# Attention feeding a dense network: another order of the first loads, of the first batch's products, and of the second batch's transposes

## The chip, the cores and the metric

The kernel runs on one core of a Trainium2 chip. Its engines are TensorE (PE in the profile; PEld is its weight load), VectorE (DVE), ScalarE (ACT), GpSimd (POOL) and SyncE (SP). All loads are issued from POOL, all stores from SP. The metric is the device time of one execution in microseconds, the median over the runs.

## The reference

For 8 batches, 8 heads, 576 positions and 64 channels a head, attention looks back over 32 positions. Heads 0 to 3 ("plain") see the last 32 positions, heads 4 to 7 ("dilated") every fourth of the last 128. The result goes, with heads side by side, through a dense network with a product of two branches.

```
rel = pos[:, None] - pos[None, :]
mask_plain = (rel >= 0) & (rel < 32)
mask_dil   = (rel >= 0) & (rel < 128) & (rel % 4 == 0)
scores = where(mask, q @ k.T / sqrt(64), -1e9)
attn = softmax(scores)
x = (attn @ v) as [8*576, 512]
out = ((x @ w1) * (x @ w2)) @ w3 @ w_out
```

w1 and w2 are 512 x 1024, w3 is 1024 x 1024, w_out is 1024 x 512.

## The kernel before

**Attention steps.** The work of a batch is cut into four steps (class Step): d0 and d1 are the two halves of the dilated heads (u = 1), p0 and p1 the two halves of the plain heads (u = 0). A step has three parts. The scores (L262 to L308): products of a k block (128 keys) with a q block (96 queries), then an exp on ACT into `et`. In the first batch the mask is added by a product with `ident` (L291); in the later ones DVE multiplies it in (L306). The values (L310 to L360): products of `et` with V, where V carries a column of ones, so that the sum of the softmax comes along; DVE takes the reciprocal (L325) and multiplies (L328) into `xo`. To channels (L366 to L388): six transposes on PE turn `xo` into the layout of the dense network, through a PSUM tile (`ps_x`, or a bank), and ACT or DVE copies that into `XT` (L388).

**q and k** come as rows. `load_qk` brings both halves u of a batch, or one; in the first batch each is a load of its own. DVE transposes them in 32 x 32 blocks (`transpose_qk`): four instructions (L247), or one for k of the plain heads (L240). Four of them take some 1.24 us.

**V** is loaded twice in two layouts: `vp` for the plain heads (one large load, and a small one of 12 KB for the first block, L130 and L131) and `vd` for the dilated heads (four loads, L140).

**The first batch** (`first_batch`, L415 to L446) is written out by hand, as nothing else can run beside it: each engine gets its instructions in the order of these lines. `scores_of_pair` and `values_of_pairs` work on two heads at a time, in two PSUM tiles `ps_s` and in banks of a pool of three (`bank()`). `begin` starts four of the dense network's products on the dilated channels of XT, which are ready first.

**The dense network and the later batches.** w3 and w_out are multiplied once into `wf_sb`: `fuse_t` transposes a block of w3 on PE and copies it to `w3T` (on DVE for odd blocks, on ACT for even ones, L593), `fuse_m` multiplies it (L601), and DVE writes the result to `wf_sb` (L609). `ffn1` (L515, L545, L546) makes the two branches for 512 tokens, `ffn2` (L571, L578) the output. Between them stand calls of `point()`, which count up. Sixteen lie in the first `ffn1` pass, two in each of the eight rounds of `fuse_m`, one ahead of each half. Steps of the second batch are due at given counts (`second_batch`, L450 to L475); those of later batches are spread evenly over the points. So instructions of a step lie in each engine's queue between those of the dense network, in the order of these calls.

**Loads** are issued in the order of the last lines of the program (L612 to L632): q, k and V of batch 0, then w1 and w2 in three parts, w3 in four, w_out in two, and the q, k and V of batch 1 among them. `const_pool` makes masks and the identity on POOL, so it stands in the same queue; `const_spread` copies masks on DVE.

Of the kernel before, what the change touches and what calls it, by code (L numbers as in the profile page):

```python
# [11 lines left out]
BF16 = mybir.dt.bfloat16  # L12
# [8 lines left out]
D = 64  # L21
# [15 lines left out]
def kernel(  # L37
# [11 lines left out]
    nc = tc.nc  # L49
# [22 lines left out]
    def four_banks():  # L72

        stage.close()
        return stage.enter_context(
            tc.tile_pool(name="psb", bufs=1, space=bass.MemoryType.PSUM)
        )
# [13 lines left out]
    NV = 3  # L91
# [8 lines left out]
    ps_x = psum.tile([P, 2 * TB], BF16, name="ps_x")  # L100
# [4 lines left out]
    def bank():  # L105
        return banks.tile([P, TB], F32, tag="f", name="f")
# [4 lines left out]
    def load_qk(b, us=slice(0, 2), which=(0, 1)):  # L111
        for nm, dst, src in [(("qn", qn, q), ("kn", kn, k))[i] for i in which]:
            if b not in dst:
                dst[b] = qk_pool.tile([P, 2, ROWS * D], BF16, tag=nm, name=nm)
            x = src[b].rearrange("(u h) (j a) d -> (h j) u (a d)", u=2, a=ROWS)
            nc.gpsimd.dma_start(out=dst[b][:, us], in_=x[:, us])  # L116

    def load_vp(b):
        vp = vps[b % NV]
        base = v[b, 0]  # L120

        def rows(p0, n, j0, nj):
            return bass.AP(
                tensor=base.tensor,
                offset=base.offset + (96 * j0 - 32 + p0) * D,
                ap=[[D, n], [96 * D, nj], [1, D]],
            )

        if b < NV:
            nc.gpsimd.dma_start(out=vp[32:P, 0:1, 0:D], in_=rows(32, 96, 0, 1))  # L130
            nc.gpsimd.dma_start(out=vp[:, 1:24, 0:D], in_=rows(0, P, 1, 23))  # L131
        else:
            nc.gpsimd.dma_start(out=vp[:, :, 0:D], in_=rows(0, P, 0, 24))

    def load_vd(b):


        x = v[b, 4]
        for m, p0, n, i0, second in ((0, 32, 96, 0, 0), (1, 0, 80, 64, 0), (1, 80, 48, 0, 1), (2, 0, P, 16, 1)):
            nc.gpsimd.dma_start(  # L140
                out=vds[b % 2][p0 : p0 + n, 4 * m : 4 * m + 4, 16 : 16 + 2 * D],
                in_=bass.AP(
                    tensor=x.tensor,
                    offset=x.offset + (4 * i0 + 2 * second) * D,
                    ap=[[4 * D, n], [S * D, 4], [1, 2 * D]],
                ),
            )
# [27 lines left out]
    def warm_up(n):  # L175

        ps = ps_x.bitcast(F32)
        for _ in range(n):
            nc.tensor.matmul(
                out=ps, lhsT=warm[:, 0:P], rhs=warm, start=True, stop=True  # L180
            )
# [19 lines left out]
    def const_pool():  # L201
        def keep(t, base, pattern, cm):
            nc.gpsimd.affine_select(
                out=t, in_=t, compare_op=AL.is_ge, fill=NEG,
                base=base, pattern=pattern, channel_multiplier=cm,
            )

        mp = mp0.rearrange("p (b a i) -> p b a i", b=2, a=2)
        keep(mp, 32, [[1, 2], [2, 2], [4, 24]], -1)
        keep(mp, -1, [[-1, 2], [-2, 2], [-4, 24]], 1)  # L210
        keep(md0, 32, [[1, 96]], -1)
        keep(md0, -1, [[-1, 96]], 1)
        make_identity(nc, ident, nomemset=True)
# [11 lines left out]
    def const_masks():  # L225
        for mask, neg in ((mask_pl, neg_pl), (mask_di, neg_di)):
            nc.vector.tensor_scalar(
                out=mask, in0=neg, scalar1=-1.0, scalar2=None, op0=AL.is_ge
            )


    def transpose_qk(b, u, which):


        src, dst = ((qn, qts), (kn, kts))[which]
        pad = PADK * which
        t = src[b][:, u, :].bitcast(U32).rearrange("p (a i) -> p a i", a=ROWS)
        o = dst[u][b % 2].rearrange("p s c -> p (s c)").bitcast(U32)[:, pad : pad + S]
        if u == 0 and which == 1:
            nc.vector.transpose(out=o.rearrange("p (j a) -> p a j", a=ROWS), in_=t)  # L240
            return
        for a0 in range(4):

            n = 5 - a0 // 2
            at = RES * SLOTS.index(a0)
            step = RES * SLOTS.index((a0 + 2) % 4) + (a0 + 18) // 4 - at
            nc.vector.transpose(  # L247
                out=bass.AP(
                    tensor=o.tensor,
                    offset=o.offset + at,  # L250
                    ap=[o.ap[0], [1, n], [9, 16], [step, 2]],
                ),
                in_=t[:, a0 : a0 + 4 * n - 3 : 4, :],
            )

    class Step:
# [80 lines left out]
        def new_xo(self):  # L337
            self.xo = wk_pool.tile([P, 2, 6, D], BF16, tag="xo", bufs=3, name="xo")

        def values_of_pairs(self):  # L340
            self.new_xo()
            products = []
            for hp in range(2):
                ov = bank()[:, 0 : 6 * (D + 1)].unsqueeze(1)
                ov = ov.rearrange("p n (j e) -> p n j e", e=D + 1)
                for m in range(3):
                    for hl in range(2):
                        self.value_matmul(2 * hp + hl, m, ov[:, 0, 2 * m + hl, :])
                products.append(self.normalize(ov, self.xo[:, hp], 1, 6))
            for f in products:  # L350
                f()

        def values(self):
# [47 lines left out]
    def prefetch(b):  # L401
        if b < B and b not in issued:
            issued.add(b)
            load_qk(b)
            load_vd(b)
            load_vp(b)

    def later(f, *args):
        phases.append([lambda: f(*args)])
# [5 lines left out]
    def first_batch():  # L415

        d0, d1, p0, p1 = steps[0:4]
        transpose_qk(0, 1, 0)
        transpose_qk(0, 1, 1)
        d0.scores_of_pair(0)  # L420
        d0.scores_of_pair(1)
        transpose_qk(0, 0, 0)
        d1.scores_of_pair(0)
        d1.scores_of_pair(1)
        d0.values_of_pairs()
        transpose_qk(0, 0, 1)
        d1.values_of_pairs()
        warm_up(4)
        p0.scores_of_pair(0)
        p0.scores_of_pair(1)  # L430
        d0.to_channels(ps_x, nc.vector.tensor_copy)
        p1.scores_of_pair(0)
        p0.values_of_pairs()
        p1.scores_of_pair(1)
        d1.to_channels()
        p1.values_of_pairs()
        pool = four_banks()
        ps_b = [pool.tile([P, TB], F32, name=f"ps_b{i}") for i in range(4)]
        begin(0, 0, ps_b[0])
        begin(0, 1, ps_b[1])  # L440
        p0.to_channels()
        begin(1, 0, ps_b[2])
        p1.to_channels(bank().bitcast(BF16), nc.vector.tensor_copy)
        begin(1, 1, ps_b[3])
        const_masks()
        prefetch(2)  # L446
# [3 lines left out]
    def second_batch():  # L450

        d0, d1, p0, p1 = steps[4:8]
        for at, f, *args in (
            (19, transpose_qk, 1, 1, 0),
            (20, transpose_qk, 1, 1, 1),
            (22, d0.scores),
            (24, d1.scores),
            (26, d0.values),
            (26, transpose_qk, 1, 0, 0),
            (27, transpose_qk, 1, 0, 1),  # L460
            (28, d0.to_channels),
            (28, d1.values),
            (30, p0.scores),
            (30, d1.to_channels),
            (32, p1.scores),
            (34, p0.values),
            (36, p0.to_channels),
            (36, p1.values),
            (36, prefetch, 3),
            (36, transpose_qk, 2, 1, 0),  # L470
            (38, p1.to_channels),
            (38, transpose_qk, 2, 1, 1),
        ):
            later(f, *args)
            when.append(at)  # L475

    def segment(lo, hi):

        for i in range(lo, hi + 2):
# [12 lines left out]
            if st is not None:  # L492
# [11 lines left out]
                if at == 3 and more:  # L504
                    behind(transpose_qk, b + 1, 0, 0)

    second_batch()
    segment(8, 4 * B)

# [15 lines left out]
    def begin(f, i, ps):  # L525

        begun[f, i] = ps
        ffn1_half(0, f, (w1_sb, w2_sb)[i], (2, 3), begun[f, i])
# [83 lines left out]
    const_vector()  # L612
    warm_up(16)
    load_qk(0, 1)
    const_pool()
    load_qk(0, 0, (0,))
    load_vd(0)
    load_qk(0, 0, (1,))
    load_vp(0)
    load_w12(0, 256)  # L620
    load_w12(256, 512)
# [8 lines left out]
    load_w3(3)  # L630
    load_qk(1, 0)
    load_vp(1)  # L632
    const_spread()

    first_batch()


# [64 lines left out]
```

## Time and profile before

| What | us |
|---|---|
| Median of 8 runs | 262.91 (262.44 to 264.09) |
| The profiled execution, its own time | 263.7 |
| Its span, first to last instruction | 261.9 |
| PE busy, of the span | 249.3 (95%) |
| DVE busy | 159.1 (61%) |
| ACT busy | 111.9 (43%) |
| Products of the dense network, first branch pair (L515) | 128.9 |
| Products of its output (L571) | 66.3 |
| Load of q of batch 1, dilated heads: issue, time to landing | 20.74, 17.6 |
| Load of k of batch 1, dilated heads | 22.07, 17.7 |

How to read it: the time of an execution is some 1.8 us over its span. PE works nearly all of the time; most of its idle time lies in the first 22 us, where the first batch waits for its loads, and between 34 and 71 us. The loads are one long stream: many are issued well before the 16 DMA engines come to them, so that the time to landing is mostly queueing.

### The profile page before, as it was taken

The numbers are of one execution on the slowest core, as the hardware profiler recorded it, in microseconds if no ns is written. First come the engines' busy times: TensorE is split into PE (matmuls) and PEld (weight loads), VectorE is DVE, ScalarE is ACT, GpSimd is POOL, SyncE is SP. The second block draws the span as 40 slices with busy tenths as digits, with TensorE's granted clock in tenths as the row PEclk, the third lists the DMA queues.
The fourth block names the chain that finished last, engine by engine and source line by source line (L and its number), as shares of the span: only waits on it lengthen the run. The fifth ranks groups of instructions, "written<-read, shape, count | busy, mean of one in ns | idle before, by whom it ended". The sixth has DMA issues, their size and how long they took to land.

```text
span 261.9 us, 5673 instructions
## 1 busy us (share of the span) xinstructions
PE 249.3 (95%) x2343; PEld 127.2 (49%) x2380; DVE 159.1 (61%) x332; ACT 111.9 (43%) x166; POOL 57.8 (22%) x84
## 2 busy tenths in 40 slices
PE   7789989999899999999999999999999999999994
PEld 2454455555455555554555555555554554444442
DVE  6575356976988578857785777578746633312420
ACT  1343334254555455345545554555445323324332
POOL 8953235546261105112411320000000000000000
PEclk9999999999999999999999999999999999999999
DMA  6999999999999969974968591300140022014013
GB/s 102 169 190 209 207 211 201 189 188 224 235 203 138 158 178 91 109 127 135 114 94 134 136 98 39 116 11 4 40 122 0 3 80 80 0 53 111 0 38 122
DMA packets 51961, 30.50 MB, mean 116 GB/s; under 512 B 37984, under 2 KB 42336, under 8 KB 51936
## 3 DMA queue, kind: packets, MB, share of 16 engines
q0 software_dynamic: 46160, 20.70, 63.7%
q1 hardware_dynamic: 5776, 9.44, 11.3%
q8 instruction: 18, 0.29, 0.4%
q14 instruction: 7, 0.06, 0.1%
HBM read 41.39 MB, written 9.44 MB: 194 GB/s over the span
## 4 chain that ended last, share of the span: by engine, by line
PE 85%; DVE 6%; DMA 2%; issue 2%; POOL 2%; ACT 2%; POOLq 0%; ACTq 0%
PE f L515 45%; PE f L571 23%; PE ps_a L275 4%; PE ps_a L317 4%; PE f L601 3%; PE ps_x L374 3%; DMA vd<-in_v_dram 2%; DVE xo L328 1%; PE ps_b L515 1%; DVE kt L240 1%; DVE qt L247 1%; ACT et L305 1%; DVE et L306 1%; POOL vd L140 1%; PE ps_s L275 1%
## 5 line engine op out<-in xcount | busy, mean ns | idle before, releaser
L515 PE MATMUL f<-XT,w_sb 128*128 128x512 bf16 x538 | 128.9, 379 | 1.3 <-issue 0.2
L515 PEld LDWEIGHTS <-w_sb 128*128 128x128 bf16 x576 | 52.8, 98 | 58.0 <-DVE XT L388 0.6
L546 DVE TENSOR_TENSOR gt<-f,asb 128x512 bf16<-128x512 f32 x70 | 48.1, 687 | 39.8 <-PE f L515 35.5
L545 ACT CAST asb<-f 128x512 bf16<-128x512 f32 x70 | 40.9, 585 | 62.6 <-PE f L515 59.8
L571 PE MATMUL f<-wf_sb,gt 128*128 128x512 bf16 (+1 forms) x287 | 66.3, 373 | 1.0 <-issue 0.8
L578 ACT COPY osb<-f 128x512 f32<-128x512 f32 (+1 forms) x37 | 21.2, 573 | 49.0 <-PE f L571 48.7
L571 PEld LDWEIGHTS <-gt 128*128 128x128 bf16 x296 | 27.1, 98 | 27.6
L305 ACT ACTIVATE et<-ps_a 128x1152 bf16<-128x1152 f32 x28 | 31.7, 1134 | 13.4 <-PE ps_a L275 13.3
L140 POOL DMA_DIRECT2D vd<-in_v_dram x32 | 21.2, 669 | 43.0 <-PE ps_a L317 35.0
L328 DVE TENSOR_TENSOR xo<-ps_a,rcp 96x768 bf16<-96x768 f32 x28 | 26.7, 954 | 1.0
L247 DVE STREAM_TRANSPOSE qt<-qn 128x160 uint32<-128x160 uint32 (+1 forms) x64 | 19.6, 423 | 1.4 <-DMA qn<-in_q_dram 1.4
L317 PEld LDWEIGHTS <-et 128*128 128x128 bf16 x384 | 15.8, 98 | 7.8 <-DVE xo L328 0.7
L275 PEld LDWEIGHTS <-kt 32*128 32x128 bf16 x768 | 10.9, 93 | 16.5 <-issue 13.1
L306 DVE TENSOR_TENSOR et<-et,mask_pl 128x1152 bf16<-128x1152 bf16 x14 | 10.6, 759 | 11.7 <-ACT et L305 11.6
L306 DVE TENSOR_TENSOR et<-et,mask_di 128x1152 bf16<-128x1152 bf16 x14 | 10.6, 757 | 10.1 <-ACT et L305 10.0
L325 DVE RECIPROCAL rcp<-ps_a 96x12 f32<-96x12 f32 x28 | 6.3, 225 | 16.4 <-PE ps_a L317 16.4
L601 PE MATMUL f<-wo_sb,w3T 128*128 128x512 bf16 x60 | 15.4, 380 | 0.9 <-ACT w3T L593 0.7
L374 PEld LDWEIGHTS <-xo 96*128 96x128 bf16 x192 | 11.4, 97 | 7.2 <-DVE xo L328 0.3
L275 PE MATMUL ps_a<-qt,kt 32*128 32x96 bf16 x672 | 12.4, 202 | 1.8 <-DVE xo L328 1.5
L374 PE MATMUL ps_x<-ident,xo 96*128 96x96 bf16 x186 | 13.1, 206 | 0.0
L116 POOL DMA_DIRECT2D qn<-in_q_dram x10 | 6.6, 663 | 21.8 <-DVE qt L247 18.1
L388 ACT COPY XT<-ps_x 128x576 bf16<-128x576 bf16 x16 | 10.3, 644 | 1.5 <-PE ps_x L374 1.4
(61 smaller groups left out, 141.9 us busy)
## 6 DMA issues: line engine op xcount, KB each, us to landing
qn<-in_q_dram POOLq DMA_DIRECT2D x6, 576.0 KB, 8.5
kn<-in_k_dram POOLq DMA_DIRECT2D x6, 576.0 KB, 9.7
w3n<-in_moe_w_dram POOLq DMA_DIRECT2D x4, 512.0 KB, 16.2
vp<-in_v_dram POOLq DMA_DIRECT2D x5, 384.0 KB, 6.5
out_dram<-osb SPq DMA_DIRECT2D x7, 256.0 KB, 2.3
out_dram<-osb SPq DMA_DIRECT2D x8, 224.0 KB, 3.1
out_dram<-osb SPq DMA_DIRECT2D x8, 192.0 KB, 2.7
out_dram<-osb SPq DMA_DIRECT2D x8, 160.0 KB, 2.3
```

The costliest lines, as they stand in the source:

```text
L140: nc.gpsimd.dma_start(out=vds[b % 2][p0 : p0 + n, 4 * m : 4 * m + 4, 16 : 16 + 2 * D], in_=bass.AP(tensor=x.tensor, offset=x.offset + (4 * ...
L275: nc.tensor.matmul(out=bank_of(h)[:, c0 : c0 + 96], lhsT=kt[prt, 96 * m : 96 * m + P, c], rhs=rhs, start=(start and c == 0), stop=(c == 1 ...
L305: nc.scalar.activation(out=ev, in_=ps_a[:, :, 0:HALF], func=ACT.Exp, scale=scale)
L306: nc.vector.tensor_tensor(out=ev, in0=ev, in1=mk.unsqueeze(1).to_broadcast([P, 4, HALF]), op=AL.mult)
L317: nc.tensor.matmul(out=out, lhsT=self.et[:, c0 : c0 + P], rhs=rhs, start=True, stop=True)
L328: nc.vector.tensor_tensor(out=xo[0:96].rearrange("p (n k) d -> p n k d", n=n), in0=ov[0:96, :, :, x0 : x0 + D], in1=rcp[0:96].unsqueeze(3) ...
L374: nc.tensor.transpose(out=xo, in_=self.xo[0:96, hp, 2 * m : 2 * m + 2, :], identity=ident[0:96, 0:96],)
L515: nc.tensor.matmul(out=ps, lhsT=w_sb[:, c, f * P : (f + 1) * P], rhs=XT[:, c, t * TB : (t + 1) * TB], start=(c == 2), stop=(c == 1),)
L545: nc.scalar.copy(out=a_sb, in_=ps)
L546: nc.vector.tensor_tensor(out=gts[t][:, f], in0=pss[1], in1=a_sb, op=AL.mult)
L571: nc.tensor.matmul(out=y, lhsT=gts[t][:, f, tb * P : (tb + 1) * P], rhs=wf_sb[:, f, c0 : c0 + n], start=(f == 0), stop=(f == KFF - 1),)
L601: nc.tensor.matmul(out=wf_ps[ft], lhsT=w3T[ft][:, g, :], rhs=wo_sb[:, g, :], start=(g == 0), stop=(g == KFF - 1),)
```

## The change

Four things are changed.

1. In the program's first loads: before, q and k of the dilated heads, the masks, q of the plain heads, V of the dilated heads (four loads), k of the plain heads, V of the plain heads. After: q and k of the dilated heads, q of the plain heads, the masks, k of the plain heads, V of the dilated heads, V of the plain heads.
2. In `first_batch`: the transposes of the plain heads' k stand ahead of d1's scores, p0's first scores ahead of d0's values, and d1's values are done in two parts between the scores of p0 and p1. Four warm-up products are gone. d0's, d1's and p0's to_channels go through `ps_x` and ACT one after the other, where d0's copy was on DVE and to_channels stood between the scores before.
3. In `second_batch`: the transposes of q and k are due at a count one higher (19, 20 to 20, 21, and 26, 27 to 27, 28), and d1's to_channels at 31 instead of 30.
4. V of the plain heads is loaded in one piece instead of two for batches 1 and 2 too (as for the later batches before).

```diff
-        if b < NV:
+        if b == 0:
             nc.gpsimd.dma_start(out=vp[32:P, 0:1, 0:D], in_=rows(32, 96, 0, 1))
             nc.gpsimd.dma_start(out=vp[:, 1:24, 0:D], in_=rows(0, P, 1, 23))
         else:
...
+        def values_of_pair(self, hp):
+            if hp == 0:
+                self.new_xo()
+            ov = bank()[:, 0 : 6 * (D + 1)].unsqueeze(1)
+            ov = ov.rearrange("p n (j e) -> p n j e", e=D + 1)
+            for m in range(3):
+                for hl in range(2):
+                    self.value_matmul(2 * hp + hl, m, ov[:, 0, 2 * m + hl, :])
+            return self.normalize(ov, self.xo[:, hp], 1, 6)
+
         def values_of_pairs(self):
...
+            for f in [self.values_of_pair(hp) for hp in range(2)]:
                 f()
...
         transpose_qk(0, 0, 0)
+        transpose_qk(0, 0, 1)
         d1.scores_of_pair(0)
         d1.scores_of_pair(1)
+        p0.scores_of_pair(0)
         d0.values_of_pairs()
-        transpose_qk(0, 0, 1)
-        d1.values_of_pairs()
-        warm_up(4)
-        p0.scores_of_pair(0)
         p0.scores_of_pair(1)
-        d0.to_channels(ps_x, nc.vector.tensor_copy)
+        d1.values_of_pair(0)()
         p1.scores_of_pair(0)
+        d1.values_of_pair(1)()
+        p1.scores_of_pair(1)
         p0.values_of_pairs()
-        p1.scores_of_pair(1)
+        d0.to_channels()
+        p1.values_of_pairs()
         d1.to_channels()
-        p1.values_of_pairs()
+        p0.to_channels()
         pool = four_banks()
         ps_b = [pool.tile([P, TB], F32, name=f"ps_b{i}") for i in range(4)]
         begin(0, 0, ps_b[0])
         begin(0, 1, ps_b[1])
-        p0.to_channels()
+        p1.to_channels(bank().bitcast(BF16), nc.vector.tensor_copy)
         begin(1, 0, ps_b[2])
-        p1.to_channels(bank().bitcast(BF16), nc.vector.tensor_copy)
         begin(1, 1, ps_b[3])
...
-            (19, transpose_qk, 1, 1, 0),
-            (20, transpose_qk, 1, 1, 1),
+            (20, transpose_qk, 1, 1, 0),
+            (21, transpose_qk, 1, 1, 1),
             (22, d0.scores),
             (24, d1.scores),
             (26, d0.values),
-            (26, transpose_qk, 1, 0, 0),
-            (27, transpose_qk, 1, 0, 1),
+            (27, transpose_qk, 1, 0, 0),
+            (28, transpose_qk, 1, 0, 1),
             (28, d0.to_channels),
             (28, d1.values),
             (30, p0.scores),
-            (30, d1.to_channels),
+            (31, d1.to_channels),
...
     load_qk(0, 1)
+    load_qk(0, 0, (0,))
     const_pool()
-    load_qk(0, 0, (0,))
+    load_qk(0, 0, (1,))
     load_vd(0)
-    load_qk(0, 0, (1,))
     load_vp(0)
```

## The prediction

> **What bounds the kernel now.** I read the page's totals first, then the chain of waits, then the timeline of the two stretches that the diff touches: 0 to 22 us (first batch of attention, alone on the chip) and 36 to 53 us (second batch, laid between products of the weights).
>
> ```profile
> PE 249.3 (95%) x2343; PEld 127.2 (49%) x2380; DVE 159.1 (61%) x332; ACT 111.9 (43%) x166; POOL 57.8 (22%) x84
> DMA  6999999999999969974968591300140022014013
> ```
>
> PE is the bound on average, so a microsecond is won or lost only where PE stands still. The DMA row shows that the 16 engines have no pause until about 90 us (14 slices of 6.55): a load's landing time is set by its place in the stream, not by when its user wants it.
>
> The chain of waits in the first stretch, and the timeline's ends of it:
>
> ```profile
> 6.48 5.63 DMA vd<-in_v_dram
> ...
> 13.69 1.17 DVE kt L240
> ...
> 21.99 1.90 PE ps_b L515 x8
> ```
>
> ```profile
> 12.15 0.59 PE L317 MATMUL f<-vd,et 128*128 128x65 bf16 x14 [0.31 <-DMA vd<-in_v_dram]
> 13.61 1.25 DVE L240 STREAM_TRANSPOSE kt<-kn 128x576 uint32<-128x576 uint32 x1
> 16.98 0.54 PE L317 MATMUL f<-vp,et 128*128 128x65 bf16 x12
> 19.48 0.98 DVE L328 TENSOR_TENSOR xo<-f,rcp 96x384 bf16<-96x384 f32 x2
> 21.98 11.77 PEld L515 LDWEIGHTS <-w_sb 128*128 128x128 bf16 x56 [0.61 <-DVE XT L388]
> ```
>
> To be seen: the last V load of the dilated heads lands at 6.48 + 5.63 = 12.11, k of the plain heads at 13.6 (issued 7.22, 6.4 to landing), and the dense products run without a break from 21.99, after the last copy into XT.
>
> The second stretch, in the timeline:
>
> ```profile
> 37.74 0.69 DVE L609 CAST wf_sb<-f 128x512 bf16<-128x512 f32 x1 [1.87 <-PE f L601]
> 37.98 1.89 PE L601 MATMUL f<-wo_sb,w3T 128*128 128x512 bf16 x7
> 38.37 1.24 DVE L247 STREAM_TRANSPOSE qt<-qn 128x160 uint32<-128x160 uint32 x4
> 39.82 1.25 DVE L247 STREAM_TRANSPOSE kt<-kn 128x160 uint32<-128x160 uint32 x4 [0.21 <-DMA kn<-in_k_dram]
> 40.90 0.68 DVE L609 CAST wf_sb<-f 128x512 bf16<-128x512 f32 x1
> 41.11 0.30 PEld L275 LDWEIGHTS <-kt 32*128 32x128 bf16 x24 [0.42 <-DVE kt L247]
> 41.49 0.68 DVE L593 COPY w3T<-f 128x1024 bf16<-128x1024 bf16 x1
> ```
>
> This one carries my forecast. q of batch 1 lands at 38.3 (issued 20.74, 17.6 to landing) and is transposed at once; k lands at 39.8 (22.07 and 17.7) and is transposed at once; the d0 scores start at 41.12, just as the transposes end at 41.07. PE has no slack to speak of here, and DVE works straight from one landing to the next. Behind it the chain goes on through PE, ACT and DVE to the p0 scores:
>
> ```profile
> 45.42 0.76 DVE et L306
> ...
> 51.38 0.96 DVE xo L328
> 52.34 0.04 issue
> 52.39 0.45 PE ps_a L275 x24
> ```
>
> From 45.42 to 52.34 DVE is filled without a gap, and PE waits 0.55 at its end. After 70.5 us no idle time of PE is over 0.16. So what d0's scores lose at 41 nothing later gives back.
>
> [...] DVE's instructions stand in the order of the code, and the 0.68 us cast at 40.90 stands behind transposes that had waited for a load. [...] The trace has the ramp (the first warm-up products stand 0.43 apart, those at 13.69 about 0.22) and no gap of PE over 0.95. [...] the early loads land in their order of issue. [...] 165 and 176 GB/s in 8 to 16 us, where V's short packets move, 206 to 212 in 20 to 40.
>
> **The change part by part.**
>
> *Load order.* Before: q1 k1 masks q0 vd(4) k0 vp; after: q1 k1 q0 masks k0 vd(4) vp. On POOL's queue q0's issue (0.55) passes the five mask selects, which so end 0.57 later, near 4.6. The mask copies on DVE (3.26 to 4.38) end near 4.95, still ahead of the first transpose at 5.49, and the identity is first wanted at 7.77: cost nothing; beyond 0.5 us it would delay that transpose. q0 can't land sooner than 9.3, since k1 (7.9) lies ahead of it. Then k0 comes next: the step from vd's last landing to k0's was 13.6 - 12.1 = 1.5, so k0 lands near 10.8 instead of 13.6, and vd's last near 9.3 + 1.5 + 2.8 = 13.6 instead of 12.1. vp (8.29 + 8.2 = 16.5) and all behind it have the same bytes ahead of them: unchanged. POOL's waits stay too: the sixth w_sb issue waited 0.3 for the load eight issues back, k0, landing at 13.6; now vd's last stands there, at 13.6 as well.
>
> *First batch.* Worked along PE. Scores of d0, d1 as before, to 11.54. DVE does q0 9.41 to 10.65 and k0 10.85 to 12.1 (1.25). p0's first scores: mask products (0.35) cover that wait, score products at 12.15 to 12.5. d0's values: four, then wait for vd until 13.6 (a new idle 0.95, in place of 0.31 + 0.54), done 13.87. Then p0's second scores (0.71) to 14.58, d1's first values (0.19) 14.77, p1's scores (0.70) 15.47, d1's second values 15.66, p1's scores 16.36. PSUM banks are free in time: the d0 products on DVE start at 13.61 + 0.56 (as 12.15 to 12.71 before) and last 0.98. p0's values need vp at 16.5: start 16.5 instead of 16.98. Now three transposes to channels use ps_x one after the other, each 0.46 to the start of ACT's copy plus 0.64 for it (20.32, 20.78, 21.42 in the trace): d0 at 16.87, d1 at 18.0, p0 at 19.13. The remaining PE work is 0.26 + 0.86 + 0.26 + 0.86 (two transposes to channels of 0.26, two pairs of begun products at four times 0.216): 21.4. DVE's last XT copy: p0's products end 18.1, p1's reciprocals and products 1.2 later, 19.3; transposed at 20.27, copied by 21.18, hidden. So dense products start at 21.4 instead of 21.99: g = 0.6 won, with both ends 0 (vp or vd 0.5 late) and 1.0 (vp not awaited). The removed warm_up(4) took 13.69 to 14.34, when PE had to wait for k0 anyway: nothing.
>
> *What the gain meets.* Weights for dense products have landed well ahead. But w3's second load lands at 36.9 (19.40 + 17.5) and its transposes ran at 37.53, so from there PE is at most 0.6 early; and the second batch's q and k still land at 38.3 and 39.8. With the old order the d0 scores would start at 41.12 whatever g is. The gain ends as idle time.
>
> *Second batch.* The k transposes move from point 20 to 21, which puts them behind the cast of wf_sb (L609) and the copy of w3T (L593) on DVE; q's from 19 to 20 moves behind one PE group only. After: q transposes at 38.39 (landing-bound as before), which issue for 1.08 (39.82 to 40.90 for four); cast 39.47, 0.59 (40.90 to 41.49); w3T copy 40.06, 0.60 (46.10 to 46.70); k transposes 40.66, 1.25 to their end at 41.91; scores 41.96. That is 41.96 - 41.12 = **0.84 later**. It needs the cast's products done by 39.47: they ended at 39.87, so g of 0.4 is enough; with g = 0 it is 0.4 more, 1.26. Queued behind: the exp, masking, d1's scores, DVE's full chain and p0's scores, all by the same 0.84. u=0's q and k transposes (26, 27 to 27, 28) only swap with one cast inside the full chain: the same sum, nothing. d1's to_channels at 31 instead of 30 removes a 0.06 pause at most; its user is hundreds of instructions off.
>
> *V of batches 1 and 2 in one load each.* One 12 KB issue (0.53 of POOL, waited 1.9 for a landing) less per batch; vp of batch 1 lands at about 52, wanted at 57: nothing.
>
> **Sum.** Profiled execution: 263.7 with span 261.9. After: -0.6 at 22 us, +0.6 idle by 37 to 41, +0.84 at 41.96: span 262.7, time 264.5. The median shown is 262.91, 0.79 under that execution; the same step on it gives 263.75, so **263.8**, 0.3% slower. About 0.3% (0.8 us) is what a measurement of this kernel can tell from no change.
>
> **Rivals.**
> 1. *Not slower: the load stream runs ahead.* If the new order of the first loads moved q of batch 1 to before 37.5 (0.84 earlier), the moved transposes would cost nothing and part of g would stay: 262.91 - 0.6 = 262.3; it decides from 0.84 on. For it: V's short packets depress the rate in 8 to 16 us. Against: the same packets are all there, and the engines had no pause to fill. 0.13.
> 2. *First batch loses as well.* vd or vp lands 0.5 late, or the serial ps_x copies on ACT take longer: g = -0.5, the casts wait for PE, 0.84 + 0.4 + 0.5 = 1.75: 264.7. For it: three copies now share ps_x and ACT, and V comes last. Against: the chain above has 0.2 us of play at begun products. 0.15.
> 3. *Partly absorbed.* The 0.55 wait at p0's scores shrinks, as DVE has already done two copies by then: +0.3, 263.2. Against: the full chain starts with the masking of d1, which moves along. 0.12.
>
> **How the numbers follow.** Forecast 0.60, its own range 263.5 to 264.4. It lies on the border: 0.43 of it over 263.7, 0.17 under. Slower: 0.43 + 0.15 = 0.58. Same: 0.17 + 0.12 + 0.05 (weak form of rival 1) = 0.34. Faster: 0.08. The range 262.9 to 264.9 leaves out most of rival 1 and the upper part of rival 2, some 0.17.
>
> **What would show it.** Right: dense products from about 21.4; w3's second transposes near 36.95, after a wait for its load; on DVE q transposes, cast, w3T copy, k transposes in that order from 38.4; PE idle some 1.5 ahead of L275 near 42.0; p0's scores near 53.2. Wrong: q of batch 1 landing more than 0.5 from 38.3, dense products after 22, or scores of d0 before 41.5.

## The result

The changed kernel takes 265.21 us in the median of 11 executions (263.78 to 268.58), the kernel before 263.0 (32 executions). The ratio is 1.0079, 95% interval 1.0061 to 1.0097: 0.8% slower; it leaves out executions more than 1.5% above the fastest of their kernel (two of the eleven, one of the 32), and the medians of the rest are 265.08 and 263.0. The forecast had the direction, and 0.3% for the size. The executions of the changed kernel differ from each other far more than those of before. The mean clock that was granted to PE, listed for each execution, goes with it: it lies between 0.972 and 1.0, where the kernel before had 0.996 or more in 41 of the 47 executions beside the first experiments. The four executions of the eleven with 0.997 or more took 263.8, 264.1, 264.7 and 265.1 (one more, listed beside them but not in the median, has 0.999 and 263.45).

The profiled execution took 265.29, span 263.5, against 263.7 and 261.9. Its page, engine totals and the clock row:

```profile
PE 248.9 (94%) x2340; PEld 127.4 (48%) x2376; DVE 158.9 (60%) x331; ACT 112.8 (43%) x167; POOL 56.5 (21%) x82
PEclk9998999999999999999999999999999999999999
```

PE is busy 0.4 us less, in a span that is 1.6 us longer: the loss is idle time and slower products, not work. Behind the first, one digit of the clock row is an 8. The table of stretches of the changed kernel shows where (columns: stretch, its length, busy time of PE, PEld, DVE, ACT and POOL with their instructions, granted clock, DMA share, GB/s):

```profile
12.00:16.00 4.00, 3.12 (x68) 1.99 (x66) 2.68 (x8) 2.56 (x4) 3.00 (x5) 1.00 1.84 172
16.00:20.00 4.00, 2.80 (x43) 2.03 (x44) 2.43 (x8) 1.91 (x3) 2.21 (x3) 0.87 1.41 195
20.00:24.00 4.00, 4.00 (x19) 1.92 (x18) 0.99 (x4) 0.58 (x1) 1.11 (x2) 0.71 1.26 208
```

The kernel before, in the same stretches from 16 on:

```profile
16.00:20.00 4.00, 3.52 (x70) 2.48 (x68) 2.55 (x9) 2.52 (x5) 2.11 (x3) 1.00 1.43 199
20.00:24.00 4.00, 3.88 (x28) 1.86 (x27) 1.97 (x5) 1.73 (x3) 1.19 (x3) 1.00 1.25 206
```

In the changed kernel's record of the clock it is whole up to 18.94, half for 3.41 us, and whole again from 22.35. A mean of 0.994 is just that: 3.41 x 0.5 / 263.5 = 0.0065. What PE did, in the changed kernel's timeline:

```profile
14.96 0.20 PE L317 MATMUL f<-vp,et 128*128 128x65 bf16 x1
16.00 0.49 PE L317 MATMUL f<-vp,et 128*128 128x65 bf16 x11 [0.83 <-DMA vp<-in_v_dram]
...
17.21 0.35 PE L317 MATMUL f<-vp,et 128*128 128x65 bf16 x6 [0.28 <-DVE xo L328]
...
18.62 0.41 PE L375 MATMUL ps_x<-ident,xo 96*128 96x96 bf16 x6 [0.73 <-ACT XT L389]
19.22 1.49 PE L516 MATMUL ps_b<-XT,w_sb 128*128 128x512 bf16 x3 [0.19 <-issue]
20.50 0.69 PE L375 MATMUL f<-ident,xo 96*128 96x96 bf16 x6
20.99 3.42 PE L516 MATMUL ps_b<-XT,w_sb 128*128 128x512 bf16 x12
24.25 0.59 PE L516 MATMUL f<-XT,w_sb 128*128 128x512 bf16 x2
```

To be seen: p0's values wait for V, and p0's to_channels for ACT's copy, as worked out ahead; then the begun dense products (the first fifteen of L516) fall for the most part into the stretch of half clock (three take 1.49 up to their modelled end). The first product in an f bank comes at 24.25; in the kernel before it came at 23.73:

```profile
23.73 3.62 PE L515 MATMUL f<-XT,w_sb 128*128 128x512 bf16 x16
```

The forecast had it 0.6 earlier than that.

The second batch, same view of the changed kernel:

```profile
38.06 0.61 PE L588 MATMUL f<-ident,w3n 128*128 128x128 bf16 x8
...
39.09 1.23 DVE L247 STREAM_TRANSPOSE qt<-qn 128x160 uint32<-128x160 uint32 x4
...
40.44 0.69 DVE L610 CAST wf_sb<-f 128x512 bf16<-128x512 f32 x1
...
41.05 0.68 DVE L594 COPY w3T<-f 128x1024 bf16<-128x1024 bf16 x1
41.64 1.20 DVE L247 STREAM_TRANSPOSE kt<-kn 128x160 uint32<-128x160 uint32 x4
...
42.67 0.44 PE L275 MATMUL ps_a<-qt,kt 32*128 32x96 bf16 x24 [0.96 <-DVE kt L247]
```

The order on DVE is the one that the forecast gave: q, cast, copy, k, and PE idle for 0.96 ahead of the d0 scores. They start at 42.67, 1.55 after those of before. And nothing behind gives it back; the chain of waits of the changed kernel:

```profile
46.98 0.76 DVE et L306
...
52.94 0.96 DVE xo L328
53.95 0.20 PE ps_a L275
```

against 45.42, 51.38 and 52.39. At the d0 scores, then, the whole difference of the two profiles stands: 1.55 of the 1.6 in the spans. How it is made up can be read from k's landing. In the profiles with the old due counts in which PE waits for k's transposes, eight in all, the d0 scores start 1.06 to 1.08 after k lands. Here k landed at 40.47 (39.80 before), so with the old order on DVE they would have started near 41.54: 0.42 of the 1.55 goes with the landing, and the other 1.13 with the cast and the copy that now stand ahead of k's transposes. That is more than the 0.84 worked out, as the cast itself started 0.27 late (40.44 instead of 39.09 + 1.08), when its products on PE were done.

### The profile page after: what moved, and what is told of

Read it like the earlier page. It is cut to its first block, busy times and chain, and to the rows that moved or that the text cites. A ratio compares the mean times of both kernels' runs of the same rounds, so it can differ in the third digit from the quotient of the medians.

```text
span 263.5 us, 5666 instructions
## 1 busy us (share of the span) xinstructions
PE 248.9 (94%) x2340; PEld 127.4 (48%) x2376; DVE 158.9 (60%) x331; ACT 112.8 (43%) x167; POOL 56.5 (21%) x82
## 3 DMA queue, kind: packets, MB, share of 16 engines
HBM read 41.41 MB, written 9.44 MB: 193 GB/s over the span
## 4 chain that ended last, share of the span: by engine, by line
PE 84%; DVE 6%; DMA 3%; POOL 2%; ACT 2%; issue 2%; POOLq 0%
PE f L516 45%; PE f L572 23%; PE ps_a L275 4%; PE ps_a L317 3%; PE f L602 3%; DMA vp<-in_v_dram 3%; PE ps_x L375 3%; PE ps_b L516 2%; DVE xo L328 1%; POOL vd L140 1%; DVE qt L247 1%; ACT et L305 1%; DVE et L306 1%; DVE wf_sb L610 1%; DVE kt L240 1%
## 5 line engine op out<-in xcount | busy, mean ns | idle before, releaser
L516 PE MATMUL f<-XT,w_sb 128*128 128x512 bf16 x538 | 128.9, 379 | 1.3 <-issue 0.2
L516 PEld LDWEIGHTS <-w_sb 128*128 128x128 bf16 x576 | 53.3, 98 | 58.4 <-issue 1.1
L389 ACT COPY XT<-ps_x 128x576 bf16<-128x576 bf16 x17 | 10.9, 644 | 2.2 <-PE ps_x L375 2.0
## 6 DMA issues: line engine op xcount, KB each, us to landing
out_dram<-osb SPq DMA_DIRECT2D x7, 256.0 KB, 2.3
```

The costliest lines, as they stand in the source:

```text
L516: nc.tensor.matmul(out=ps, lhsT=w_sb[:, c, f * P : (f + 1) * P], rhs=XT[:, c, t * TB : (t + 1) * TB], start=(c == 2), stop=(c == 1),)
```

## The experiments

Times are medians, and the ratios are to the kernel before, run beside; its medians were 263.08 to 263.14 there, so that times of different sets can be compared to about 0.1. The mean clock is listed for every execution. A mean down to 0.996 is called whole here: it can come from the end of the program, where PE has little to do (in one profile half clock from 260.79 to the end, at 262.4: 0.997). Timelines and landings come from the one execution of each kernel that was profiled.

**The due counts, undone and alone.** In the changed kernel, back to before:

```diff
-            (20, transpose_qk, 1, 1, 0),
-            (21, transpose_qk, 1, 1, 1),
+            (19, transpose_qk, 1, 1, 0),
+            (20, transpose_qk, 1, 1, 1),
...
-            (27, transpose_qk, 1, 0, 0),
-            (28, transpose_qk, 1, 0, 1),
+            (26, transpose_qk, 1, 0, 0),
+            (27, transpose_qk, 1, 0, 1),
...
-            (31, d1.to_channels),
+            (30, d1.to_channels),
```

> The changed kernel with the second batch's due counts of before (19, 20; 26, 27; d1's to_channels at 30); nothing else. Theory (three causes: due counts, clock, landing of q and k): the d0 scores wait for q landing + 1.1 + k's transposes alone, so they start 0.6 to 0.9 us sooner than in the changed kernel for the same landing, and the time falls by as much, from 265.2 to about 264.5, a ratio of 1.005 to 1.006 to before; clock below 1 in some runs as before. Rival (the clock alone makes the loss): no change, 265.2, ratio 1.008. Rival (the due counts alone): 263.0, ratio 1.000.

Measured: 264.75, ratio 1.0056 (1.0035 to 1.0077). The interval overlaps that of the changed kernel, as the clock still scatters the times. By mean clock the 22 executions fall into steps: 263.3 in the median of seven at 0.997 or more, 264.7 in that of six near 0.985, 266.1 in that of six near 0.978. So a mean of 0.985 goes with 1.4 us more than a whole clock, and one of 0.978 with 2.8, and with a whole clock this kernel is within 0.2 of before (263.3 against 263.14). In its profile, where V happened to land at 14.70, the first product in an f bank came at 21.91, 1.8 before that of the kernel before; its span was 261.4.

The opposite edit, the new due counts in the kernel before:

> The kernel before with the second batch's due counts of the changed one; nothing else. Theory: on DVE q's transposes, then a cast that waits for its products (39.9), a copy, then k's transposes: the d0 scores start near 42.1 instead of 41.1, all later work 1.0 us later: 264.0, ratio 1.004, clock whole in all runs. Rival (clock alone, due counts free): 263.0, ratio 1.000.

Measured: 264.06, ratio 1.0025 (1.0009 to 1.0041), clock whole in 21 of 22. The due counts alone cost 264.06 - 263.14 = 0.92 us of the medians. (Its profiled d0 scores stood at 41.54 and not at 42.1, the time expected, as q had landed at 37.4, a microsecond sooner than in the profile of before.)

**The warm-ups.** In the changed kernel one set put back, and in the kernel before the set taken out:

```diff
         p1.scores_of_pair(1)
+        warm_up(4)
         p0.values_of_pairs()
```

> The changed kernel with warm_up(4) put back, ahead of p0's values, where PE waits 0.8 us for V. Theory: the clock stays whole between 15 and 24 us in most runs, dense products start near 23.5 or sooner instead of 24.25 (the first product in an f bank), the spread shrinks to that of before, and the time falls by 0.7 to 1.2 us, to 264.0 to 264.5, ratio 1.004 to 1.006. Rival (due counts or landings alone): clock whole, but the time stays at 265.2, as the second batch waits anyway for its k.

```diff
         d1.values_of_pairs()
-        warm_up(4)
         p0.scores_of_pair(0)
```

> The kernel before without its warm_up(4); nothing else. If the removal of these products is what lets the clock fall: clock 0.98 to 0.997 in some runs and 263.5 to 265, ratio over 1.002. If it is the idle time that the new order of the first batch makes between 15 and 19 us: clock whole, 263.0, ratio 1.000.

Measured: 264.66, ratio 1.0051 (1.0019 to 1.0083), for the first, with a clock of 0.996 or more in seven of ten; its profiled execution is one in which the clock fell, at 14.34, before the warm-ups at 17.4. That is above the expected 264.5, and the interval overlaps that of the changed kernel: one set in one place doesn't hold the clock. For the second: 265.44, ratio 1.0075 (1.0046 to 1.0104), clock 0.981 to 0.993 in all six, more than the 263.5 to 265 expected. In the kernel before, taking out four products, and nothing else, costs as much as the whole change. The stretches and the timeline of the kernel before without its warm-ups:

```profile
12.00:16.00 4.00, 2.63 (x42) 1.60 (x42) 3.21 (x8) 1.30 (x2) 3.69 (x6) 0.88 1.88 176
16.00:20.00 4.00, 4.00 (x58) 2.96 (x58) 1.68 (x6) 1.83 (x3) 1.95 (x4) 0.50 1.42 197
```

```profile
13.97 0.43 PE L275 MATMUL ps_s<-qt,kt 32*128 32x96 bf16 x12 [1.13 <-DVE rcp L325]
14.33 0.42 PE L291 MATMUL ps_s<-neg_pl,ident 128*128 128x288 bf16 x2
14.68 0.43 PE L275 MATMUL ps_s<-qt,kt 32*128 32x96 bf16 x12
15.05 0.66 PE L374 MATMUL ps_x<-ident,xo 96*128 96x96 bf16 x6
15.51 0.68 PE L291 MATMUL ps_s<-neg_pl,ident 128*128 128x288 bf16 x2
```

There is a wait of 1.13 where the warm-ups had been, and from 15.05 the same two mask products take 0.68 up to their modelled end instead of 0.42. The first product in an f bank came at 25.14 instead of 23.73.

**Warm-ups in all of the first batch's waits**, in the changed kernel, with the old due counts and with the new:

```diff
-    def warm_up(n):
+    def warm_up(n, ps=None):
 
-        ps = ps_x.bitcast(F32)
+        ps = ps_x.bitcast(F32) if ps is None else ps
...
+        warm_up(2)
         p0.scores_of_pair(0)
...
+        warm_up(4)
         p0.values_of_pairs()
...
+        warm_up(1, ps_s[0][:, 0])
         d1.to_channels()
+        warm_up(3, ps_s[0][:, 0])
         p0.to_channels()
```

> The changed kernel with the due counts of before and with ten warm-up products laid in the waits of its first batch (two ahead of p0's first scores, four ahead of p0's values, one ahead of d1's and three ahead of p0's to_channels). Theory [...] the clock is whole in at least nine runs of ten, and the time is that of the whole-clock runs of the changed kernel with the old due counts, 263.0 to 263.5: ratio 0.999 to 1.002. Rival (the clock falls for another reason, and warm-ups don't hold it): clock under 0.99 in half the runs, 264.7, ratio 1.005. If the first batch's gain were not held up by the second batch's loads: 262, ratio 0.996.

> The same with the changed kernel's own due counts. Theory: clock whole, so only the due counts are left of the loss: 0.8 to 1.0 over the kernel with the old counts beside it, 263.9 to 264.3, ratio 1.003 to 1.005. Rival (clock alone makes the loss): 263.1, ratio 1.000. Rival (warm-ups don't hold the clock): 265, ratio 1.008.

Measured: 263.76, ratio 1.0014 (1.0000 to 1.0028), and 264.41, ratio 1.0037 (1.0025 to 1.0049). The clock was 0.997 or more in all 33 executions, as expected, against 7 of 22 and 4 of 11 without the ten products. So what PE does in the waits of the first batch decides whether the clock falls. Both times lie over their expected ranges, by 0.3 and 0.1, and the difference of the two is under the 0.8 to 1.0 expected. Of the changed kernel's 2.2 us, 265.21 - 264.41 = 0.8 go with the clock (0.7 from the 265.08) and 264.41 - 263.76 = 0.65 with the due counts, as the timelines of DVE and of the d0 scores in the two show, old due counts first:

```profile
38.97 1.22 DVE L247 STREAM_TRANSPOSE qt<-qn 128x160 uint32<-128x160 uint32 x4 [0.60 <-DMA qn<-in_q_dram]
40.36 1.23 DVE L247 STREAM_TRANSPOSE kt<-kn 128x160 uint32<-128x160 uint32 x4 [0.17 <-DMA kn<-in_k_dram]
41.41 0.44 PE L275 MATMUL ps_a<-qt,kt 32*128 32x96 bf16 x24 [0.21 <-DVE kt L247]
41.43 0.67 DVE L614 CAST wf_sb<-f 128x512 bf16<-128x512 f32 x1
```

```profile
38.94 1.23 DVE L247 STREAM_TRANSPOSE qt<-qn 128x160 uint32<-128x160 uint32 x4 [1.10 <-DMA qn<-in_q_dram]
40.00 0.69 DVE L614 CAST wf_sb<-f 128x512 bf16<-128x512 f32 x1
40.59 0.69 DVE L598 COPY w3T<-f 128x1024 bf16<-128x1024 bf16 x1
41.18 1.22 DVE L247 STREAM_TRANSPOSE kt<-kn 128x160 uint32<-128x160 uint32 x4
42.23 0.44 PE L275 MATMUL ps_a<-qt,kt 32*128 32x96 bf16 x24 [1.06 <-DVE kt L247]
```

q lands at the same time in both (38.95 and 38.91); k's transposes start 0.82 later with the new counts, and PE's d0 scores at 42.23 instead of 41.41. That is the forecast's 0.84, in isolation.

What is left is 263.76 - 263.13 = 0.63 over the kernel before, with whole clock and old due counts. Three things could make it: the landings of the loads, the new order of the products, and the ten warm-ups. In the profile with the old counts DVE waits for q and then for k, and the d0 scores start 1.08 after k's landing at 40.33. From the d0 scores to the end every one of the 17 profiles has the same 222.6 to 223.0 us. So in this execution (264.2) the landing alone sets the time; PE, with its new order and its warm-ups, waits. Why the loads land late is another question. The same kernel without the ten warm-ups had 263.3 in its seven executions of whole clock, and no run tells whether warm-ups move the landings; among the kernels with work left out, below, eight more of them did not (263.16 against 263.13).

**The load order, alone and undone.** The last lines of the diff only, in the kernel before, and taken back in the changed one:

> The kernel before with the changed order of its first loads alone. Theory: k of the plain heads lands 2.5 us sooner and V of the dilated heads 1.5 us later; d0's values, and all behind them on PE, start about 1.5 us later in the old order of products, k's transpose comes before them; dense products start within 0.8 us of 23.7 on either side, and the loads of the second batch hold the d0 scores near 41 anyway. [...] the clock falls in some runs: 263.1 to 264.5, ratio 1.000 to 1.005. If the load order does harm later (q of batch 1 lands later): q of batch 1 over 38.6 and ratio over 1.003 at whole clock.

> The changed kernel with the order of the first loads of before. Theory: p0's first scores wait for k (landing 12.6 to 13.6 instead of 10.2) and hold up d0's values behind them, so PE stands still 1.5 to 2.5 us longer between 11 and 14; the clock falls in most runs; due counts cost as in the changed kernel: 265.2 to 267, ratio 1.008 to 1.015. Rival (load order is a cause of the loss): 264 or less, ratio under 1.005.

Measured: 265.38, ratio 1.0073 (1.0048 to 1.0099), and 269.67, ratio 1.0235 (1.0213 to 1.0257). Both are above what was expected, 264.5 and 267 at most. In both, the order of products and that of loads don't fit each other, PE waits, and the clock falls: under 0.995 in six of seven executions, and under 0.983 in all five (13.65 us of half clock in the second one's profile). They say that the two halves of the change belong together, and next to nothing on what the loads do later: the first had a single execution of whole clock, 263.82.

**What holds the second batch.** In the kernel before, twelve of the dense products are left out (half the channels of f = 5, 6, 7 for the first 512 tokens), so that PE comes to the second batch 2.6 us sooner:

```diff
-                ffn1_half(t, f, w_sb, (2, 3, 0, 1), ps)
+                ffn1_half(t, f, w_sb, (2, 1) if t == 0 and f >= 5 else (2, 3, 0, 1), ps)
```

> The kernel before with twelve dense products left out (half the channels of f = 5, 6, 7 for the first 512 tokens), 2.6 us of PE ahead of the weight products, so that the second batch waits for its loads and for nothing else. Theory (loads hold the second batch): only part of the 2.6 is won: the d0 scores start 1.0 to 1.1 after k of batch 1 lands, 39.8 to 40.9, and the time is 262.0 to 262.9, ratio 0.996 to 0.999. Rival (PE holds it): 260.5, ratio 0.990.

Measured: 263.13, ratio 0.9994 (0.9978 to 1.0011): of 2.6 us nothing comes through, where 0.2 to 1.1 was expected. PE's timeline of this kernel:

```profile
36.41 0.62 PE L587 MATMUL f<-ident,w3n 128*128 128x128 bf16 x8 [0.79 <-DMA w3n<-in_moe_w_dram]
...
40.29 0.44 PE L275 MATMUL ps_a<-qt,kt 32*128 32x96 bf16 x24 [0.22 <-DVE kt L247]
```

It waits for w3's second load and then for k. So what the new order of the first batch wins could not have shown in the median, whatever its size, as long as the loads land when they do.

The same work left out, with other orders of the first loads, and warm-ups (six ahead of d0's values, six in the place of the four) so that the clock holds:

> The same twelve products left out, with the changed order of the first loads and twelve warm-ups in two places in place of four, to hold the clock. Both this kernel and the one without the new load order wait for the loads of the second batch, so their difference is what the load order does to those landings. Theory (the order moves the first loads only; which of the 16 DMA engines is last is chance): within 0.2 us of the other, ratio 0.996 to 0.999. Rival (the new order makes the slowest DMA engine later for good): 0.5 to 0.9 us slower than the other, ratio 0.998 to 1.002.

> As the kernel with the twelve products left out, the new load order and twelve warm-ups, but the masks stand ahead of q of the plain heads as before: of the load order only k's move ahead of V is left. If that move (V's short packets of both layouts now follow each other) makes the slowest DMA engine late: q of batch 1 lands at 38.3 or later and the time is 263.4 to 263.7. If not: q lands near 37.7, 263.1.

> The same with k behind V as before, and q of the plain heads ahead of the masks: the other half of the new load order. If k's move is the cause: q of batch 1 lands near 37.7, 263.1. If q's earlier issue is the cause: 38.3 or later, 263.4 to 263.7.

> The same with the load order of before: twelve products left out and twelve warm-ups. It takes the warm-ups out of the comparison: if they did the harm, 263.5; if the load order did it, 263.1 and q of batch 1 near 37.7.

| Order of the first loads | Median, us | Ratio (interval) | q of batch 1 lands (time of that execution) |
|---|---|---|---|
| as before, twelve warm-ups | 263.16 | 1.0000 (0.9981 to 1.0019) | 37.79 (263.18) |
| q ahead of the masks only | 263.35 | 1.0002 (0.9983 to 1.0022) | 39.03 (264.24) |
| k ahead of V only | 263.59 | 1.0015 (0.9998 to 1.0031) | 38.23 (263.45) |
| both, as in the change | 263.52 | 1.0012 (1.0002 to 1.0021) | 39.05 (264.27) |

The clock was whole in all 72 executions. The last column is the one profiled execution, with its own time behind; in all four the time is the landing plus 225.2 to 225.4, so here the landing sets it. Two of the four happened to be late ones, 0.8 to 0.9 over their median, so the landings in the column can't be compared with each other, and the medians can. With k ahead of V they are 0.4 higher than with the old order, which lies between what the two sides of the first expectation gave (0.2 at most, or 0.5 to 0.9); q alone gives 0.2; taken together, the 44 executions with k ahead have a median of 263.55 and the 28 others 263.27. The intervals overlap, so k's move is what it points to and isn't shown, and q's part stays open: with q alone the profile landed late and the median hardly moved. Of all 17 profiles, the eight with k ahead of V have q of batch 1 landing at 37.9 to 39.1, mean 38.6; the nine with k behind V at 37.3 to 39.0, mean 37.8; other edits differ among them too. How that comes can be seen in the completion of the single DMA engines for that load:

```
q of batch 1, us       8th of 16   15th   last engine
before                   36.1      37.4    38.3
changed                  36.1      37.6    39.1
before, new due counts   36.2      37.3    37.4
```

The median engine is the same within 0.1 in these three. The last engine is 0.9 and 1.5 behind the 15th in the first two and 0.1 in the third, and the load has landed only when it is done. Which engine falls behind, and why the order has to do with it, was not found.

**V of batches 1 and 2 in one load, alone**, in the kernel before:

> The kernel before with V of the plain heads in one load for batches 1 and 2; nothing else. Theory: free, V lands 4 us or more before it is wanted: 263.1, ratio 0.999 to 1.001. Rival (it shifts later loads): over 1.002.

Measured: 263.21, ratio 0.9997 (0.9986 to 1.0009). Free, as forecast.

**More warm-ups in the kernel before** (one ahead of d0's values, two ahead of d1's values, five in place of four):

> The kernel before with eight warm-ups in place of four (one ahead of d0's values, two ahead of d1's values, five in the old place). Theory: the few runs of before whose clock falls go away; those with a whole clock stay within 0.3 us, as the second batch's loads take up what the first batch loses: median 263.0 to 263.3, ratio 0.999 to 1.001, and no run over 264.5. Rival (warm-ups cost what they take): 0.9 us more, ratio 1.003.

Measured: 263.07, ratio 0.9999 (0.9984 to 1.0014); a clock under 0.996 in one of 22 executions, against 5 of 59 of the kernel before beside it, too few to tell apart. Four more products cost nothing. That one execution took 266.15, so the expected bound of 264.5 was missed. No version beats the kernel before by more than can be measured.

## Why the forecast was wrong

*Due counts: right.* The step "That is 41.96 - 41.12 = 0.84 later" holds: 0.92 alone in the kernel before, 0.65 in the medians and 0.82 at the d0 scores with the clock held. Nothing later gave it back. One reading under it was off: the d0 scores of the kernel before were taken as held by k's transposes, but k was ready at 39.80 + 1.07 = 40.87, and PE came 0.25 later on its own account.

*The gain meets the loads: right.* The kernel with 2.6 us less work shows it without any other change. And in the profile of the changed kernel with the old due counts, PE was 1.8 earlier at the first product in an f bank (21.91), and its d0 scores waited for k all the same, by 0.23.

*The clock, put at nothing: this is the step that failed.* The forecast said of the removed warm-ups "when PE had to wait for k0 anyway: nothing", and kept PE at full clock through the waits of its new order. The four products cost no time where they stood; what they did was hold the clock. Alone, their removal costs 2.3 us (265.44 against 263.14). In the changed kernel the clock is 0.8 in the medians, and it makes most of the scatter; how much of this is the removal and how much the new waits was not told apart, as one set put back didn't hold the clock. The forecast looked for the longest gap of PE, 0.95, and left the clock out of every rival; in the changed kernel the clock fell with no gap over 0.83. The forecast should have added up the gaps that it worked out itself (0.95 ahead of d0's values, and the waits at ps_x): in the 3.41 us before the fall at 18.94, PE streamed columns for 0.39 of the time.

*Landings: a second miss.* "unchanged" was wrong for what lies behind vp: the bytes ahead of it are the same, but the last of 16 DMA engines is later, by 0.7 in the two profiles compared (38.34 and 39.07). That is the forecast's own sign of being wrong, q of batch 1 more than 0.5 from 38.3. Among the kernels with work left out, those with k ahead of V are some 0.3 to 0.4 us slower, which points to the order and doesn't show it. The landings of the first loads themselves were 0.5 to 1.5 sooner than worked out (q of the plain heads at 8.37, k at 10.15, V of the dilated heads at 12.15). That fits with the one profile that the forecast worked from, which was a late one: k of the dilated heads landed at 7.89 there, and at 6.72 to 7.05 in all sixteen others.

*Sum, in medians.* Due counts 0.65, clock 0.8, the remaining 0.63: 2.1 of 2.2. The clock and the remainder, 0.8 + 0.63, are about what the forecast missed, 265.21 - 263.8 = 1.4. Of the remainder, some 0.4 is what the kernels with work left out point to for the new order of the loads, and 0.2 no run told apart.

The rival "first batch loses as well" had 264.7 and came nearer, by luck: its g of -0.5 is what the profile has (24.25 against 23.73 for the first product in an f bank), but PE there was not late because V or the copies were; its products took twice as long (at half clock they start 0.43 apart, 19.22 to 19.65, and at whole clock 0.22, 22.52 to 22.74).

## What to carry to other kernels

A filler product that costs no time can still be doing work (here four of them, taken out, cost 2.3 us): before it is taken out, or gaps are opened between short products, look at the granted clock of all executions, not only at the idle time. Where a stream of loads holds a later stage, as here, what earlier stages win may not arrive (2.6 us of products less: ratio 0.9994); leaving work out ahead of it is a quick test. Before moving an instruction in an engine's queue, read which waiting instructions it comes to stand behind (the due counts alone cost 0.92 us here). And landing times of one profile are one draw (37.3 to 39.1 here for the same load): compare a few before working out tenths from them.

## What the runs showed of the hardware

*The clock fell at 18.94 with no gap of PE over 0.83 behind the start.* The trace of the changed kernel has whole clock from 5.28 for 13.653 us, half clock for 3.413, and whole clock for 242.346; that of the kernel before has whole clock from 7.26 for 256.0. These are 4, 1, 71 and 75 times 3.413. Half clock of 6.8 us is in the trace of the kernel before without its warm-ups, and of 13.65 in that of the changed one with the old loads, 2 and 4 times 3.413. The first warm-up product starts at 1.46 in the first two, so the first change stood at another point in each. From the traces I added up, in stretches of 3.413 us counted from these changes, the time in which PE streams columns (512 columns in 0.427 us at half clock, as the first warm-up products follow each other in the traces, and half of that at whole clock; overlaps counted once):

```
stretch of 3.413 us from      share  clock in the next stretch
 9.8  before, new loads        0.29   half
11.6  before, no warm-ups      0.34   half
 9.1  changed, old loads       0.34   half
10.9  changed, one warm-up set 0.38   half
13.0  before, less work        0.47   half
15.5  changed                  0.39   half
 8.7  changed                  0.53   whole
10.7  before                   0.47   whole
11.8  before, new due counts   0.49   whole
14.2  changed, old due counts  0.51   whole
```

The share of time alone doesn't sort them: 0.47 stands on both sides, and in the trace of the kernel before the clock was whole after the stretch from 256.4 too, which has 0.43. What does was not shown. The shares put a size to the warm-ups: four of them, at 4 x 0.216 us, are an estimated 0.25 of a stretch, and the stretch of the kernel before from 10.7 has 0.47 with two of them in it, that of the kernel without them 0.34. Why the same kernel loses none, one or several stretches in different executions (the changed one fell below 0.997 in 7 of 11, the changed one with the old due counts in 15 of 22, the kernel before below 0.996 in 5 of 59) was not shown either.

*The last of sixteen DMA engines set the landing.* Up to 3 us lie between the median and the last engine (36.1 and 39.1 above), and the landing is the last one's: DVE starts on q at 38.37 in the profile of before and at 39.09 in that of the changed kernel, 0.03 and 0.02 behind it. In eight profiles the d0 scores follow k's landing by 1.06 to 1.08 us, so that a late engine is paid in full.
